# A long-convolution layer and a SwiGLU layer on one core: block 1's v loaded early into a y buffer, loads reordered, down weights in two pieces, opening planned anew

## The chip, the cores and the metric

The kernel runs on one core of a Trainium2 chip. The core has a matrix engine (PE, with its weight loads shown apart as PEld), a vector engine (DVE), an activation engine (ACT), a general engine (POOL) and a queue engine (SP) that issues transfers; 16 DMA engines move the data. The metric is device time in microseconds of one execution. Before the change the median of 13 runs is 350.85 us (349.63 to 352.18).

## The reference

Inputs are q, k, v of 2048 positions by 512 channels, a shift kernel of 4 taps and a long kernel of 2048 taps for each channel, and three weight matrices of a gated feed-forward layer (512 by 1792 twice, 1792 by 512). Everything is bf16. With x = q, two layers run, each of the form:

```python
x = x + A(layernorm(x), k, v)      # A: k_shift = 4-tap causal convolution of k
                                   #    kv = k_shift * v
                                   #    y = causal convolution of kv with ssm_k (by FFT) + kv * ssm_D
                                   #    returns layernorm(x) * y
x = x + B(layernorm(x))            # B: (silu(z @ w_gate) * (z @ w_up)) @ w_down
```

A's y doesn't depend on x: both layers use the same y, which is computed once. Only the normalised x that multiplies it differs.

## The kernel before, in words

The 2048 positions are cut into four blocks (c = 0 to 3) of 512. A block's convolution is done with transforms of 1024 points as matrix products: `spectrum_h` and `spectrum_x` bring a block of the long kernel and of kv to frequencies (H, X), `fold_h` combines two neighbouring kernel blocks to G, `product(i, j)` multiplies X of block i with G of block j on DVE and adds into Z of block i + j, and `inverse` brings Z back to y on PE. The opening does the same for block 0 in a shorter form (`half`, `direct`, `inverse_half`).

The feed-forward part runs in 16 units (layer, block, half), in the order of blocks, then layers, then halves. For 14 tiles of hidden features PE forms gate and up products into `pf` (112 matmuls of 256 columns for a unit), ACT applies Silu (`sg`) and copies the up part (`ht`), DVE multiplies both (line 903), and PE multiplies by the down weights into `pd` (line 916, 28 matmuls of 512 columns). `prologue(layer, c, h)` stands ahead of each unit: it normalises x, multiplies by y, adds, normalises again into z, and turns z into zT, in the first unit by PE (line 850, with copies by ACT and by DVE in line 853), in the others by transposing transfers that SP issues (line 827).

Nothing is issued in the order of the program. Each operation is recorded with its engine, an estimated cost, for transfers an estimated landing time (`lat`), and what it reads and writes (class `Plan`). `dues` gives each a due time, from the units' planned starts (`T0`, `DUR`) and slacks (`SLK`, `HSL`, `ASL`), stretched by group (`STRETCH`) and moved one by one by `SHIFTS`. `forward` then plays the estimates and so fixes one order for each engine's queue; at run time each engine works through its queue and waits on semaphores. `warm` puts small matmuls into planned holes of PE before 32 us. The lists `ST1`, `ST2`, `N_ACT`, `Z_ACT` say for which units statistics and normalisations run on ACT and not on DVE; `X_PE` says for which units x is added in `pd` by a matmul with the identity (line 875) instead of by DVE (line 955).

Buffers are rings: a load into a ring waits until the buffer's former readers are done. Ring `v` has one buffer, ring `y` two, `s8` ten. Block 1's v (`vt`) shares the one `v` buffer with block 0's, which PE reads until 21.3 us (line 468). Its 4-tap product with k is on DVE in line 519, from ACT's copy `ks` (line 518) of PE's shifted k. All transfers but one are issued by SP, one after the other; each uses one of eight semaphores in turn, and waits for the transfer eight before it. In the opening SP issues, in this order: taps, k of block 0, D, v of block 0, x of block 0, h of block 1, gate weights, the first half of the inverse table (a transposing transfer, line 1038), k of block 1 (transposing, line 370), down weights, the second half of the table, up weights, v of block 1 (line 396), then x, h and k for the next blocks.

Of the kernel before, what the change touches and what calls it, by code (L numbers as in the profile page):

```python
# [9 lines left out]
P = 128  # L10
# [3 lines left out]
ACT = mybir.ActivationFunctionType  # L14
# [2 lines left out]
LN_EPS = 1e-5  # L17

NB = 4
SLK = 25.57  # L20
H_DMA = lambda b: b in {2, 3}
ST1 = lambda l, c, h: (l, c, h) in {(0, 2, 0), (0, 3, 0), (1, 0, 0)}
ST2 = lambda l, c, h: (l, c, h) in {(0, 0, 0), (0, 2, 1), (1, 2, 1), (1, 3, 1)}
ASL = -167.89
K_ACT = lambda b: b in {2, 3}
PASSES = 1
PW = 1.2
PD_ACT, KV_ACT, ST_ACT = True, True, False
HSL = 49.11
Z_ACT = lambda l, c, h: (l, c, h) in {(0, 0, 1), (0, 3, 1), (1, 0, 0), (1, 0, 1), (1, 1, 1), (1, 2, 1)}  # L30
N_ACT = lambda l, c, h: (l, c, h) in {(0, 2, 0), (0, 3, 0), (1, 0, 1), (1, 1, 1), (1, 3, 0)}
GROUPS = (4, 4, 4, 2)
TINY = 0.2
SHIFTS = {8: -168.0, 9: -2.0, 32: -48.0, 36: -20.0, 48: -11.0, 50: -14.0, 52: 81.0, 66: -34.0, 67: 46.0, 70: 119.0, 78: 4.0, 83: 4.0, 89: 13.0, 99: 167.0, 102: 22.0, 106: -52.0, 109: -49.0, 130: 36.0, 136: 21.0, 161: 56.0, 176: -79.0, 186: -34.0, 240: 10.0, 241: 11.0, 248: 184.0, 250: 53.0, 258: -67.0}
X0, H0, I0 = 'direct', 'half', 'half'
Z_DUE = -45
X_PE = lambda l, c, h: (l, c, h) in {(0, 0, 0), (1, 2, 0)}
RINGS = {}
T0, FLOOR = 25.95, -54.39
DUR = [27.46, 52.65, 71.28, 66.57, 24.46, 6.54, 42.65, 47.17, 9.57, 39.07, 58.13, 31.81, 76.24, 78.5, 43.25, 33.23]  # L40
STRETCH = {1: {'PE': 2.47, 'DVE': 5.84, 'ACT': 16.37, 'POOL': 2535.84, 'SP': 127809.23}, 2: {'PE': 6.24, 'DVE': 2.14, 'ACT': 0.5, 'POOL': 1.22, 'SP': 3.69}, 3: {'PE': 13.63, 'DVE': 2.09, 'ACT': 1.5, 'POOL': 0.74, 'SP': 5.68}}
R = 4


# [230 lines left out]
def kernel(  # L275
# [14 lines left out]
    nc = tc.nc  # L290
    _, S, D = A_q.shape
# [25 lines left out]
    def new(ring, name, shape, dtype=BF16, parts=1):  # L317
        space = psp if ring in ("pf", "pc", "pd") else pool

        def make(slot):  # L320
            tag = f"{ring}{slot}" if ring != "one" else name
            return space.tile(list(shape), dtype, name=name, tag=tag)
        return plan.buf(ring, name, make, parts)

    def whole(name, shape, dtype=BF16, parts=1):
        return new("one", name, shape, dtype, parts)
# [20 lines left out]
    tapT, drow = whole("tapT", [P, KD, KS]), new("jk", "drow", [P, D])  # L347
    dg = whole("dg", [P, KD, KS, P], parts=KD * KS)
    fwd, inv = whole("fwd", [P, NT, P], parts=4), whole("inv", [P, NT, P], parts=2)
    wt = {"g": whole("wg_sb", [P, KD, F]), "u": whole("wu_sb", [P, KD, F]), "d": whole("wd_sb", [P, NF, D])}  # L350

    def fT(f, r):
        return fwd.t[:, BI[f, r], :]
# [11 lines left out]
    def load_k(b, due=None, after=()):  # L365
        if b == 0:
            kn[b] = new("s8", "kn", [P, R, D])
            return add("SP", 0.5, lambda: nc.sync.dma_start(out=kn[b].t[:], in_=k_t[:, b]), w=[kn[b]], lat=4.6, due=due)
        kT[b] = new("s8" if b == 1 else "k", "kTb", [P, KD, PADL + L])
        add("SP", 5.0 if b == 1 else 2.2, lambda: nc.sync.dma_start_transpose(out=kT[b].t[:], in_=k3[b * L - PADL:(b + 1) * L]),  # L370
            w=[kT[b]], lat=7.0 if b == 1 else 8.0, due=due, after=after)

    def transpose_k(b, ring, engs):

# [17 lines left out]
        return k_in  # L392

    def load_v(b, due=None, after=()):
        vt[b] = new("v", "vt", [P, R, D], parts=R)
        return add("SP", 0.6, lambda: nc.sync.dma_start(out=vt[b].t[:], in_=v_t[:, b]), w=[vt[b]], lat=4.5 if b else 5.9, due=due, after=after)

    def load_x(c, due=None, after=()):
        xs[c] = new("x", "xc", [P, R, D], parts=R + 2)
# [2 lines left out]
    def load_weights(which, due, after=()):  # L402
        if which in ("g", "u"):
            src = (B_w_gate if which == "g" else B_w_up).rearrange("(k p) f -> p k f", p=P)
        else:
            src = B_w_down.rearrange("(k p) d -> p k d", p=P)
        return add("SP", 0.6, lambda: nc.sync.dma_start(out=wt[which].t[:], in_=src), w=[wt[which]], lat=12.0, due=due, after=after)


    X, G, H, Y, Z = {}, {}, {}, {}, {}  # L410
# [451 lines left out]
    def ffn(unit):  # L862
# [18 lines left out]
        for fts in groups:  # L881
            n = len(fts)
            sg = new("sg", "sg", [P, n, W], parts=n // 2)
            ht = new("ht", "ht", [P, n, W], parts=n // 2)
            for o in range(0, n, 2):
                for which in ("g", "u"):
                    ps = new("pf", "pf", [P, D], F32)

                    def go(ps=ps, o=o, which=which, fts=fts):
                        for q in (0, 1):  # L890
                            ft = fts[o + q]
                            mm(ps.t[:, q * W:(q + 1) * W],
                               [(wt[which].t[:, kd, ft * P:(ft + 1) * P], zT.t[:, kd]) for kd in range(KD)])
                    add("PE", pe(2 * KD, W), go, r=[zT, wt[which]], w=[ps], due=(unit, (k + (which == "u") / 3) / pairs, 0.0, None))
                    if which == "g":
                        add("ACT", act(D), lambda ps=ps, o=o, sg=sg: nc.scalar.activation(  # L896
                            out=sg.t[:, o:o + 2, :], in_=ps.t[:], func=ACT.Silu), r=[ps], w=[(sg, (o // 2,))],
                            due=(unit, k / pairs, 1.0, "a"))
                    else:
                        add("ACT", act(D), lambda ps=ps, o=o, ht=ht: nc.scalar.copy(out=ht.t[:, o:o + 2, :], in_=ps.t[:]),  # L900
                            r=[ps], w=[(ht, (o // 2,))], due=(unit, k / pairs, 1.5, "a"))
                k += 1
            dve(n * W, lambda sg=sg, ht=ht: nc.vector.tensor_mul(out=ht.t[:], in0=ht.t[:], in1=sg.t[:]), [sg], [ht],  # L903
                due=(unit, k / pairs, 0.0, "h"))
            for o in range(HP):
                i = HP * h + o
                last = unit == LAST_UNIT and fts[-1] == NF - 1 and o == HP - 1
                split = unit == LAST_UNIT and o == HP - 1
                halves = (slice(0, D // 2), slice(D // 2, D))
                cols = [[cs] for cs in halves] if last else [halves] if split else [[slice(0, D)]]  # L910

                for css in cols:
                    def go(o=o, fts=fts, ht=ht, css=css):
                        for cs in css:
                            for q, ft in enumerate(fts):
                                nc.tensor.matmul((pds[o] if not cs.start else pds[HP]).t[:, cs], lhsT=ht.t[:, q, o * P:(o + 1) * P], rhs=wt["d"].t[:, ft, cs],  # L916
                                                 start=(ft == 0 and not xpe), stop=(ft == NF - 1))
                    add("PE", pe(n) if not last else pe(n, D // 2), go, r=[ht, wt["d"]],
                        w=[pds[o]] if not split else [pds[o], pds[HP]] if not last else [pds[HP if css[0].start else o]],
                        due=(unit, k / pairs, 2.0, None))  # L920
        if unit == LAST_UNIT:
# [81 lines left out]
            out=fwd.t[:, dst, :], in0=fwd.t[:, src, :], scalar1=-1.0, scalar2=None, op0=ALU.mult),  # L1003
            r=[(fwd, (n,))], w=[(fwd, (part,))])
    h1 = load_h(1, "SP", -57.5, after=[x0])
    wg = load_weights("g", -57, after=[h1])
    hs = transpose_h(0, "pf", (0, 2, 1, 3), False, ("DVE", "ACT"), drow)
    ev = spectrum("ev")
    if H0 == "half":
# [25 lines left out]
    k_in = transpose_k(0, "pc", ("ACT", "DVE"))  # L1035
    for n in range(2):
        sl = slice(n * NI, (n + 1) * NI)
        tabs = add("SP", 4.0, lambda sl=sl: nc.sync.dma_start_transpose(
            out=inv.t[:, sl, :], in_=fwd.t[:, sl, :].rearrange("p k f -> p (k f)")), r=[fwd], w=[(inv, (n,))], lat=5.5, due=-56.8,
            after=[wg, k_in])  # L1040
    load_k(1, -56.4, after=[tabs])
    load_weights("u", -56, after=[tabs])
    load_weights("d", -55, after=[tabs])
    shift_mul(0, "pf", False, due=-49)
    normed[0, 0, 0] = apply_norm(0, 0, on_act=True, due=-47)
    if H0 == "half":
# [24 lines left out]
        product(0, 0, [slot], False)  # L1071
    plan.grp = 1
    spectrum_h(1, "pf")
    v1 = load_v(1, after=[turned[1]] if 1 in turned else ())
    plan.grp = 0
    if I0 == "half":
        inverse_half(0, (0, 1))
# [16 lines left out]
    def conv(c):  # L1094
        if c >= NB:
            return
        plan.grp = c
        if c > 1:
            spectrum_h(c)
        fold_h(c)  # L1100
        spectrum_x(c)
        load_x(c, after=[v1])
        if c + 1 < NB:
            gate = list(first) if c == 1 else ()
            load_h(c + 1, after=gate)
            load_k(c + 1, after=gate)
            load_v(c + 1, after=gate)
        product(0, c)
        product(c, 0)
        inverse(c)  # L1110
        for i in range(1, c + 1):
            if i + c < NB:
                product(i, c)
                if i != c:
                    product(c, i)
# [53 lines left out]
```

## Time and profile before

| | us |
|---|---|
| median of 13 runs | 350.85 |
| the profiled execution: its time | 351.87 |
| the profiled execution: its span | 350.1 |
| busy in the span: PE, DVE, ACT, POOL | 340.2, 280.5, 259.6, 39.5 |
| first matmul of the first unit | 35.78 |
| longest wait of PE | 2.2 |
| loads issued, and time to landing: gate weights | 3.32, 12.1 |
| up weights | 21.09, 10.5 |
| v of block 1 | 21.79, 11.1 |

The profile is of one execution, taken by the hardware profiler. Its times count from the start of the span. A line of the list of waits gives who waited for whom, the sum, how often, and the longest. A line of the chain gives start, duration, engine and line, and how many instructions follow each other. A line of the timeline gives start, duration, engine, line, operation, output and inputs, shape and count, and in brackets the idle time before it with what ended it. PE's ends are modelled, so starts of neighbours say more than durations. The page's row PEclk is the clock that PE was granted, in tenths, in 40 equal slices. A few records of matmuls are missing from such a trace.

### The profile page before, as it was taken

To read this page: it belongs to the slowest core of one execution; us is meant where nothing else is said; L and a number is where in the kernel's file an instruction comes from. 1 tells how busy PE (TensorE), PEld (TensorE's weight loads), DVE (VectorE), ACT (ScalarE), POOL (GpSimd) and SP (SyncE) were. 2 spreads that over 40 slices of the span, in tenths; PEclk is the share of its full clock that TensorE was granted. 3 is DMA by queue.
4 is the path that set the end of the run, shared out by engine and by line. 5 is a ranking of instruction groups with operands and counts; after the bars stand their busy time and mean duration, and the time that the engine had idled before them with its cause. 6 is when DMAs were issued, how large, how long until landed. Compare 5 with 4: busy or idle time off the path is not lost.

```text
span 350.1 us, 6568 instructions
## 1 busy us (share of the span) xinstructions
PE 340.2 (97%) x2582; PEld 249.4 (71%) x2608; DVE 280.5 (80%) x471; ACT 259.6 (74%) x507; POOL 39.5 (11%) x46
## 2 busy tenths in 40 slices
PE   7997999999999999999999999999999999999996
PEld 7664676858588685858586777758586877777684
DVE  7897979999998997899999999999997523643120
ACT  6996896758779994938896989859983755648460
POOL 4100100111132000201212001101201000100000
PEclk9999699999999999999999999999999999999999
DMA  8999202010251116310113040120101130000200
GB/s 290 310 318 325 48 29 63 2 32 0 44 137 34 25 19 140 110 42 2 30 34 78 16 119 2 36 56 0 33 30 25 39 32 0 17 15 2 61 2 30
DMA packets 42073, 22.96 MB, mean 66 GB/s; under 512 B 33845, under 2 KB 39866, under 8 KB 42042
## 3 DMA queue, kind: packets, MB, share of 16 engines
q1 hardware_dynamic: 41370, 21.95, 24.3%
q10 hardware_dynamic: 672, 0.59, 0.6%
q8 instruction: 20, 0.33, 0.4%
q14 instruction: 11, 0.09, 0.1%
HBM read 12.33 MB, written 2.10 MB: 41 GB/s over the span
## 4 chain that ended last, share of the span: by engine, by line
PE 75%; DVE 13%; ACT 5%; DMA 4%; issue 2%; POOL 0%; DVEq 0%; POOLq 0%; ACTq 0%
PE pf L338 44%; PE pd L916 21%; PE ps L338 5%; DMA vt<-in_A_v_dram 3%; PE ps L468 2%; DVE ht L903 2%; DVE bnst L743 1%; DVE t L655 1%; DVE t L651 1%; DVE t L663 1%; ACT ht L900 1%; DVE ka L606 1%; PE wm L1135 1%; ACT sg L896 1%; DMA zT<-z 1%
## 5 line engine op out<-in xcount | busy, mean ns | idle before, releaser
L338 PE MATMUL pf<-zT,wg_sb 128*128 128x256 bf16 x896 | 117.8, 275 | 1.1 <-DVE zT L853 0.6
L338 PE MATMUL pf<-zT,wu_sb 128*128 128x256 bf16 x896 | 117.0, 274 | 0.0
L338 PEld LDWEIGHTS <-wg_sb 128*128 128x128 bf16 x896 | 88.1, 99 | 20.1 <-issue 1.3
L916 PE MATMUL pd<-wd_sb,ht 128*128 128x512 bf16 (+1 forms) x446 | 97.9, 372 | 1.2 <-DVE ht L903 0.3
L338 PEld LDWEIGHTS <-wu_sb 128*128 128x128 bf16 x896 | 88.1, 98 | 13.2
L896 ACT ACTIVATE sg<-pf 128x512 bf16<-128x512 f32 x112 | 67.3, 602 | 18.9 <-PE pf L338 17.6
L916 PEld LDWEIGHTS <-ht 128*128 128x128 bf16 x462 | 45.0, 98 | 47.4 <-DVE ht L903 0.9
L900 ACT CAST ht<-pf 128x512 bf16<-128x512 f32 x112 | 65.8, 587 | 15.1 <-PE pf L338 14.2
L903 DVE TENSOR_TENSOR ht<-ht,sg 128x1024 bf16<-128x1024 bf16 (+1 forms) x64 | 39.4, 620 | 26.9 <-ACT ht L900 26.9
L748 POOL TENSOR_TENSOR rstd<-ve,nhalf 128x2 f32<-128x2 f32 x24 | 27.5, 1146 | 219.3 <-DVE ve L746 205.5
L952 ACT CAST dn<-pd 128x512 bf16<-128x512 f32 x26 | 14.1, 591 | 34.5 <-PE pd L916 34.5
L743 DVE BATCH_NORM_STATS2 bnst<-xc 128x6 f32<-128x512 bf16 x48 | 31.4, 686 | 0.7
L651 DVE TENSOR_TENSOR t<-X,G 128x2048 bf16<-128x2048 bf16 x18 | 21.9, 1219 | 0.1
L655 DVE TENSOR_TENSOR t<-X,G 128x2048 bf16<-128x2048 bf16 x18 | 21.9, 1218 | 0.0
L955 DVE TENSOR_TENSOR xc<-xc,dn 128x1024 bf16<-128x1024 bf16 x13 | 8.9, 688 | 15.4 <-ACT dn L952 15.4
L429 ACT ACTIVATE X<-ps 128x512 bf16<-128x512 f32 x32 | 17.8, 603 | 0.2
L820 DVE TENSOR_TENSOR n<-n,Yk 128x1024 bf16<-128x1024 bf16 x15 | 10.4, 691 | 5.7 <-ACT n L793 3.8
L665 DVE TENSOR_TENSOR Z<-Z,t 128x2048 bf16<-128x2048 bf16 x12 | 14.7, 1222 | 0.2
L429 ACT ACTIVATE H<-ps 128x512 bf16<-128x512 f32 x24 | 13.2, 616 | 2.2 <-PE ps L338 2.1
L663 DVE TENSOR_TENSOR t<-t,t 128x2048 bf16<-128x2048 bf16 x12 | 14.6, 1220 | 0.1
L774 POOL TENSOR_TENSOR rstd<-ve,nhalf 128x2 f32<-128x2 f32 x8 | 7.8, 981 | 59.6 <-ACT ve L772 59.6
L768 ACT ACTIVATE jk<-xc,nm 128x512 bf16<-128x512 bf16 x16 | 11.5, 720 | 0.3
(108 smaller groups left out, 318.6 us busy)
## 6 DMA issues: line engine op xcount, KB each, us to landing
vt<-in_A_v_dram SPq DMA_DIRECT2D x4, 512.0 KB, 8.5
xc<-in_A_q_dram SPq DMA_DIRECT2D x4, 512.0 KB, 5.2
out_dram<-xc SPq DMA_DIRECT2D x15, 128.0 KB, 1.8
wg_sb<-in_B_w_gate_dram SPq DMA_DIRECT2D x1, 1792.0 KB, 12.1
wd_sb<-in_B_w_down_dram SPq DMA_DIRECT2D x1, 1792.0 KB, 8.2
wu_sb<-in_B_w_up_dram SPq DMA_DIRECT2D x1, 1792.0 KB, 10.5
hn<-in_A_ssm_k_dram SPq DMA_DIRECT2D x3, 512.0 KB, 7.9
hn<-in_A_ssm_k_dram ACTq DMA_DIRECT2D x1, 512.0 KB, 3.6
```

The lines of the kernel that those rows point to most:

```text
L338: nc.tensor.matmul(o, lhsT=lhsT, rhs=rhs, start=(n == 0), stop=(n == len(terms) - 1))
L429: add("ACT", act(D), lambda: nc.scalar.activation(out=view(), in_=ps.t[:], func=ACT.Copy, scale=scale), r=[ps], w=[(buf, keys)], conv=conv)
L651: dve(n * D, lambda t1=t1, part=part: nc.vector.tensor_mul(out=t1.t[:], in0=x.t[:, sl, 0, :], in1=g.t[:, sl, part, :]), [(x, key(slots, (0 ...
L655: dve(n * D, lambda t2=t2, part=part: nc.vector.tensor_mul(out=t2.t[:], in0=x.t[:, sl, 1, :], in1=g.t[:, sl, 1 - part, :]), [(x, key(slots ...
L663: dve(n * D, lambda t1=t1, t2=t2, comb=comb: nc.vector.tensor_tensor(out=t1.t[:], in0=t1.t[:], in1=t2.t[:], op=comb), [t2], [t1], conv=conv)
L665: dve(n * D, lambda t1=t1, part=part: nc.vector.tensor_add(out=z.t[:, sl, part, :], in0=z.t[:, sl, part, :], in1=t1.t[:]), [t1], [zk], con ...
L743: add("DVE", 0.6, lambda st=st, i=i: nc.vector.bn_stats(out=st.t[:], in_=xs[c].t[:, i, :]), r=[(xs[c], (i,))], w=[st])
L748: add("POOL", pw, lambda: nc.gpsimd.tensor_tensor(out=rstd.t[:], in0=ve.t[:], in1=nhalf.t[:].to_broadcast((P, n)), op=ALU.pow), r=[ve, nha ...
L896: add("ACT", act(D), lambda ps=ps, o=o, sg=sg: nc.scalar.activation(out=sg.t[:, o:o + 2, :], in_=ps.t[:], func=ACT.Silu), r=[ps], w=[(sg, ...
L900: add("ACT", act(D), lambda ps=ps, o=o, ht=ht: nc.scalar.copy(out=ht.t[:, o:o + 2, :], in_=ps.t[:]), r=[ps], w=[(ht, (o // 2,))], due=(uni ...
L903: dve(n * W, lambda sg=sg, ht=ht: nc.vector.tensor_mul(out=ht.t[:], in0=ht.t[:], in1=sg.t[:]), [sg], [ht], due=(unit, k / pairs, 0.0, "h"))
L916: nc.tensor.matmul((pds[o] if not cs.start else pds[HP]).t[:, cs], lhsT=ht.t[:, q, o * P:(o + 1) * P], rhs=wt["d"].t[:, ft, cs], start=(ft ...
```

## The change

Block 1's v gets a buffer of ring `y`, and its load is placed after h of block 1 and ahead of the gate weights. Both halves of the inverse table are now issued one after the other, ahead of k of block 1; then follow the up weights, and the down weights in two pieces (the first four feature tiles, then ten), which the down matmuls wait for separately. Landing times in the plan get new values. All the plan's constants and lists change with it, so each engine's order is another one through the whole kernel. On SP the opening's order is now: k of block 0, taps, D, v of block 0, x of block 0, h of block 1, v of block 1, gate weights, both halves of the table, k of block 1, up weights, the two pieces of the down weights, x of block 1, h, k and v of block 2. The warm-up matmuls go from 23 to 28, with 6 more ahead of H of block 1; `X_PE` gets the units (0, 0, 1) and (0, 2, 1).

```diff
-SLK = 25.57
+SLK = 22.46
-ST1 = lambda l, c, h: (l, c, h) in {(0, 2, 0), (0, 3, 0), (1, 0, 0)}
-ST2 = lambda l, c, h: (l, c, h) in {(0, 0, 0), (0, 2, 1), (1, 2, 1), (1, 3, 1)}
-ASL = -167.89
+ST1 = lambda l, c, h: (l, c, h) in {(0, 0, 0), (0, 1, 0), (0, 2, 0), (0, 3, 0), (0, 3, 1), (1, 0, 0)}
+ST2 = lambda l, c, h: (l, c, h) in {(0, 0, 0), (0, 2, 1), (1, 2, 1)}
+ASL = -171.35
-HSL = 49.11
-Z_ACT = lambda l, c, h: (l, c, h) in {(0, 0, 1), (0, 3, 1), (1, 0, 0), (1, 0, 1), (1, 1, 1), (1, 2, 1)}
-N_ACT = lambda l, c, h: (l, c, h) in {(0, 2, 0), (0, 3, 0), (1, 0, 1), (1, 1, 1), (1, 3, 0)}
+HSL = 66.69
+Z_ACT = lambda l, c, h: (l, c, h) in {(0, 2, 0), (0, 3, 1), (1, 0, 0), (1, 1, 0), (1, 1, 1), (1, 3, 0)}
+N_ACT = lambda l, c, h: (l, c, h) in {(0, 2, 1), (0, 3, 0), (0, 3, 1), (1, 1, 1), (1, 3, 1)}
-SHIFTS = {8: -168.0, 9: -2.0, 32: -48.0, ...
+SHIFTS = {11: 77.0, 31: 6.0, 34: -33.0, ...
-X_PE = lambda l, c, h: (l, c, h) in {(0, 0, 0), (1, 2, 0)}
+X_PE = lambda l, c, h: (l, c, h) in {(0, 0, 0), (0, 0, 1), (0, 2, 1), (1, 2, 0), (1, 3, 1)}
-T0, FLOOR = 25.95, -54.39
+T0, FLOOR = 85.74, -22.82
...
-"d": whole("wd_sb", [P, NF, D])}
+"d": whole("wd_sb", [P, NF, D], parts=2)}
...
-        vt[b] = new("v", "vt", [P, R, D], parts=R)
+        vt[b] = new("y" if b == 1 else "v", "vt", [P, R, D], parts=R)
...
+            for part, sl in enumerate((slice(0, GROUPS[0]), slice(GROUPS[0], NF))):
+                o = add("SP", 0.6, lambda sl=sl: nc.sync.dma_start(out=wt[which].t[:, sl], in_=src[:, sl]), w=[(wt[which], (part,))],
+                        lat=(8.0, 11.5)[part], due=due, after=after)
+            return o
...
-                    add("PE", pe(n) if not last else pe(n, D // 2), go, r=[ht, wt["d"]],
+                    add("PE", pe(n) if not last else pe(n, D // 2), go, r=[ht, (wt["d"], (0 if fts[0] == 0 else 1,))],
...
     h1 = load_h(1, "SP", -57.5, after=[x0])
-    wg = load_weights("g", -57, after=[h1])
+    v1 = load_v(1, -57.2, after=[h1])
+    wg = load_weights("g", -57, after=[v1])
...
-    load_k(1, -56.4, after=[tabs])
-    load_weights("u", -56, after=[tabs])
-    load_weights("d", -55, after=[tabs])
+    k1 = load_k(1, -56.4, after=[tabs])
+    wu = load_weights("u", -56, after=[k1])
+    wd = load_weights("d", -55, after=[wu])
...
-    v1 = load_v(1, after=[turned[1]] if 1 in turned else ())
...
-        load_x(c, after=[v1])
+        load_x(c, after=[wd])
```

## The prediction

> **What bounds the kernel now.** I read the page's first lines, then PE's waits, the chain, a table by stage, and the timelines.
>
> The page and its row of granted clock:
>
> ```profile
> PE 340.2 (97%) x2582; PEld 249.4 (71%) x2608; DVE 280.5 (80%) x471; ACT 259.6 (74%) x507; POOL 39.5 (11%) x46
> PEclk9999699999999999999999999999999999999999
> ```
>
> PE is the bound, with one hole: the fifth slice (35 to 44 us) has the clock at 6 tenths.
>
> PE's waits, and the chain:
>
> ```profile
> PE ptz L850 <- ACT ks L518: 2.2, 1, 2.2
> PE pf L338 <- DVE zT L853: 0.6, 1, 0.6
> ...
> 21.79 11.11 DMA vt<-in_A_v_dram
> 33.00 0.44 DVE vt L519
> 34.14 1.05 PE ptz L850 x8
> 35.78 7.89 PE pf L338 x48
> ```
>
> PE's long wait is one. The chain says what is behind it: block 1's v, issued at 21.79, lands at 32.9; the DVE product that needs it stands ahead of the two z of the first FFN unit.
>
> By stage (columns: stretch, then busy us of PE, PEld, DVE, ACT, POOL, then granted clock, DMA share, GB/s):
>
> ```profile
> 21.30:31.80 10.50, 10.32 (x106) 7.00 (x105) 9.21 (x21) 8.75 (x16) 0.69 (x1) 1.00 1.07 372
> 31.80:35.80 4.00, 1.19 (x10) 0.82 (x10) 2.66 (x8) 2.29 (x5) 0.00 (x0) 0.79 1.29 191
> 35.80:41.00 5.20, 5.20 (x25) 3.60 (x26) 5.13 (x7) 4.44 (x13) 1.03 (x1) 0.51 0.25 58
> 150.00:252.00 102.00, 101.19 (x737) 72.44 (x743) 100.97 (x149) 83.57 (x170) 13.36 (x10) 1.00 0.16 37
> 252.00:350.00 98.00, 94.20 (x722) 71.12 (x729) 43.13 (x86) 56.65 (x107) 6.45 (x8) 1.00 0.11 23
> ```
>
> Up to 35 us the DMA engines are full. After the hole PE runs 5.2 us at half clock. From 150 to 252 DVE is as full as PE, so whatever arrives late on DVE there decides too.
>
> PE's and DVE's timelines:
>
> ```profile
> 37.44 1.91 PE L338 MATMUL pf<-zT,wu_sb 128*128 128x256 bf16 x8
> 39.15 1.91 PE L338 MATMUL pf<-zT,wg_sb 128*128 128x256 bf16 x8
> 41.77 1.04 PE L338 MATMUL pf<-zT,wg_sb 128*128 128x256 bf16 x8
> 42.64 1.04 PE L338 MATMUL pf<-zT,wu_sb 128*128 128x256 bf16 x8
> ...
> 138.30 0.69 DVE L955 TENSOR_TENSOR xc<-xc,dn 128x1024 bf16<-128x1024 bf16 x1 [1.88 <-ACT dn L952]
> 228.00 0.73 DVE L798 TENSOR_SCALAR z<-xc,mv,rstd 128x512 bf16<-128x512 bf16 x2
> ```
>
> Eight matmuls take 1.71 us (37.44 to 39.15) and later 0.87 (41.77 to 42.64): the halved clock, in the record.
>
> **The change part by part.** Sums go against the profiled execution: span 350.1, its time 351.87, which is 1.0 above the median 350.85; I subtract differences from the median.
>
> *v of block 1 early.* It goes from thirteenth to seventh in SP's queue and is issued near 3.4. Before, v0, x0 and h1 landed at 7.8, 9.2 and 10.6 (5.9, 6.9 and 7.9 after issue): 1.4 us per 512 KB. So v1 lands near 12, over 17 us before its use. What it passes comes 1.4 us later: wg 16.8 instead of 15.4 (12.1 from 3.32), wanted at 34; the other transfers have their own line below. The order shows a new wait on wg, for the first h load (landed 4.3); wg is then issued 1 us later, covered by the same 17 us. With the wait gone, next in line on DVE are the statistics: ve ends 30.9, rstd takes 0.69 on POOL, so z could start near 31.8 instead of 33.7.
>
> *Warm-up matmuls, 23 to 28 and 6 more.* Five at 0.114 (2.63 for 23) put off the transposes by up to 0.57; at 6.8 the clock rises, which returns half: I take 0.4. The six stand in a hole that waits for ACT's copy of h: zero; without that cover 6 x 0.056 = 0.3.
>
> *PE's order up to the first FFN.* The same instructions, regrouped. From the end of the h1 transposes (22.2, now 22.6) stand 8 + 16 + 2 matmuls of 0.216, 64 tap matmuls of 0.06 to 0.065, eight transposes of 0.056: 9.9 to 10.2, and some 1.75 of waits: 0.8 for ACT's first copy of h, 0.3 and 0.55 for DVE's m, 0.1 for z. So PE, no longer DVE, sets the start: 34.4 instead of 35.78, **-1.4**, with the zT copy at 33.9 instead of 35.2.
>
> *The clock.* The largest hole I find on PE is now some 0.6 us against 2.4 before, so no half clock: the 24 matmuls from 35.78 to 40.86 take 24 x 0.109 = 2.6 instead of 5.1, **-2.5**. The Trainium skill ("TensorE: Matmul & The Clock Gate", Why this matters for your kernels) asks only to avoid idle gaps over about 3 us. Here 2.4 us was followed by the halving, so the trace is stricter; by the page's rule the change would have nothing to win here, and the sum would be 2.5 worse.
>
> *Transposes of the inverse tables and k.* Now consecutive on SP: 5.1 + 4.3 + 6.1 from 5.2 on, so k of block 1 is fully issued near 20.8 instead of 16.1. Its landing isn't shown before. Block 2's landed 2.7 after SP was done (14.2 from 23.84, 11.5 on SP), the first table 6.3 after: 23.5 to 27.1. PE wants it near 24.1: zero to +3.0. I take zero, since little is queued ahead of it then; the upper end stays in the range. wu follows: issued 21.1 as before, 10.5 to land at most, 31.6, wanted at 36.
>
> *wd in two pieces.* One more issue on SP (0.59) ahead of x1, h2, k2, which nobody wants before 70 us: zero. Its parts land at the latest with the old last load of this stretch, 36 to 38, wanted near 43 and 48. v2 now waits for v0's readers (done by 21.3) and no longer for v1's, so it can't hold the zT transposes behind it.
>
> *The y slot.* Y0 has the other slot; Y1 needs one only after X1 is formed (50.2 before) and is written past 80 us: zero.
>
> *X_PE on two more units.* Two matmuls each, 4 x 0.216 = **+0.9** on PE. DVE loses two adds of 0.69.
>
> *ST, Z, N lists and the new order.* In all DVE has -2.9 us, ACT +3.1 (two sums and two squares of rows more, 0.71 to 0.81 each; ACT has 83.6 of 102 us busy in the full stretch, which covers them). Place matters more than totals. I summed DVE's instructions in list order, each at the spacing of its row, from the zT copy to the second z of unit (layer 1, block 2, half 0), just where before has no slack (z ends 228.7, zT lands 232.46, PE starts 232.59). Before: 287 instructions, 184.5 us, done in 193.5, so 9.0 were idle. After: two products more (2 x 1.135), one ht (0.60), two n (0.73), less two bn with their small ones (1.56) and one add (0.69): 185.8. Of the 9.0 idle, the 1.88 at 138.3 waits for PE, and PE is ahead now: I take 7.1. Then z ends 33.9 + 185.8 + 7.1 = 226.8, zT lands 3.8 later at 230.6. PE's matmuls up to that unit are 194.2 (193.3 and the 0.9): 228.6. It waits 2.0, where before it had lost 0.9 by then: **+1.1**. The ends: 9.0 idle costs +3.0, 5.1 or less costs -0.9. Past 252 DVE is at 43 of 98 us and hides its part.
>
> Sum: -1.4 - 2.5 + 0.9 + 1.1 = -1.9: span 348.2, time **348.9**.
>
> The page "DMA: Bandwidth & Descriptors" (Issuing engines are not separate DMA queues) says all loads interleave on the same 16 engines, so an early load is paid by others. The trace agrees (DMA share 1.07 to 35 us); by the slack in the sums above, only k pays.
>
> **The rivals.**
>
> *DVE gives nothing back* (the new order fits the earlier PE): PE alone counts, -1.4 - 2.5 + 0.9 and up to -0.5 for a faster start: 347.3 to 347.8. For it: DVE totals fall by 2.9 and past this unit the sums are 1.6 to 6 smaller than before. Against: between 150 and 252 DVE has 1 us free of 102.
>
> *DVE takes everything* (the slower side): the order asks 4 to 6 us more of DVE ahead of the products ht of units (1,1,0) and (1,1,1), and if DVE then also stands idle for PE or ACT as it did, 9.0 us, z ends at 228.7 as before: no change, 350.8. From 9.7 idle it decides for slower, 1 us for each: with 11, 352.8. For it: static order, 83.6 of 102 on ACT and 3.1 more to come. Against: the waits of 35 to 150 hang on PE, which is ahead.
>
> *The opening stalls again* (k late by up to 3.0, a hole like the old one, half clock 2.5): gain gone, 350.5 to 352.
>
> *v1 was hidden anyway*: no; its landing ends the only long wait of PE. Without any effect of it the time would be 350.85 + 0.9.
>
> **How the numbers follow.** A change under 0.2% (0.7 us) can hardly be told from none. Forecast 0.42 (own range 347.9 to 350.1); nothing given back 0.20; DVE as idle as before, no change, 0.12; DVE more idle, slower, 0.16; opening stalls, slower, 0.10. Faster 0.62, same 0.12, slower 0.26. The range reaches down to a start at 33.9 without any stall, 346.9, and up to the late k or 10.4 us idle, 352.2.
>
> **What would show it.** Right: v1 landing near 12; no PE hole over 1 us between 22 and 35; clock 9s in the fifth slice; first pf near 34.4; PE waiting about 2 us in all before the unit (1,2,0), for ht or zT. Wrong: PE waiting on taps for k near 24; a 5 or 6 in PEclk; many PE waits for DVE's ht between 40 and 60 or 160 and 230, in all over 4 us; the ACT queue late for sg and ht in the first unit, which the half clock used to cover.

## The result, and the profile after

The changed kernel takes 347.46 us (median of 11 runs, 347.22 to 349.50) against 350.72 (48 runs, 349.38 to 352.22): a ratio of 0.9922, interval 0.9904 to 0.9939. The forecast was 348.9. A twelfth execution was disturbed (2048 us), and it was the profiled one; so the lines of the changed kernel below are of the same kernel, unaltered, profiled again in a later run (e9 below: span 345.6, its time 347.32).

The times of the changed kernel don't spread evenly. Over this series and two later ones (e1 and e9), 23 executions without the disturbed one, 14 lie between 347.2 and 348.3, most of them at 347.2 to 347.5, and 9 between 349.1 and 349.7. The profile below is one of the 14; e1's is one of the 9.

The page, its busy times and the row of granted clock:

```profile
PE 337.5 (98%) x2595; PEld 248.6 (72%) x2623; DVE 277.4 (80%) x465; ACT 262.3 (76%) x515; POOL 39.6 (11%) x46
PEclk9999999999999999999999999999999999999999
```

The hole in the fifth slice is gone. So is PE's wait of 2.2 us for v; its list of waits begins, apart from the start of the kernel, with small ones:

```profile
PE ps L338 <- ACT hs L495: 0.4, 1, 0.4
PE pt L1025 <- DMA tapR<-in_A_shift_k_dram: 0.3, 1, 0.3
PE ps L338 <- ACT X L433: 0.3, 1, 0.3
PE pt L491 <- DMA hn<-in_A_ssm_k_dram: 0.2, 1, 0.2
```

Two of these, for the taps and for the first h, stand in the first six microseconds; they come up again.

The chain of work that ended last (start, duration, engine and line) no longer has a transfer of v in it; between 30 and 33 us it goes:

```profile
30.09 1.05 PE ps L338 x16
31.15 0.05 issue
31.20 1.24 PE ps L735 x5
32.44 0.24 PE ptz L854 x4
32.70 0.58 ACT zT L859
```

PE's own work runs into the transposes of z without a hole. By stage, in the stretches that were used before (the last one shorter, as the span is):

```profile
21.30:31.80 10.50, 9.77 (x106) 6.96 (x107) 10.07 (x24) 9.41 (x18) 0.80 (x1) 1.00 1.06 376
31.80:35.80 4.00, 4.00 (x36) 2.93 (x35) 3.97 (x8) 3.90 (x11) 0.00 (x0) 1.00 1.24 221
35.80:41.00 5.20, 5.15 (x47) 4.48 (x46) 5.17 (x7) 4.92 (x12) 1.67 (x1) 1.00 0.37 108
150.00:252.00 102.00, 101.58 (x759) 74.76 (x765) 98.40 (x147) 87.43 (x176) 14.81 (x11) 1.00 0.16 37
252.00:345.00 93.00, 89.84 (x688) 67.71 (x692) 37.17 (x78) 55.50 (x103) 5.13 (x7) 1.00 0.09 21
```

The granted clock is 1.00 in every row, where it was 0.79 and 0.51 in two of them. From 150 to 252 us DVE has 98.4 busy us where it had 101.0. PE's and DVE's timelines around the first FFN matmul, and one later add:

```profile
32.28 0.61 PE L854 MATMUL ptz<-ident,z 128*128 128x128 bf16 x8
32.72 0.38 PE L735 MATMUL ps<-m,inv 128*128 128x512 bf16 x1
32.94 0.59 PE L879 MATMUL pd<-xc,ident 128*128 128x512 bf16 x2
33.49 1.03 PE L338 MATMUL pf<-zT,wg_sb 128*128 128x256 bf16 x8
34.36 1.04 PE L338 MATMUL pf<-zT,wu_sb 128*128 128x256 bf16 x8
```

```profile
31.55 0.74 DVE L802 TENSOR_SCALAR z<-xc,mv,rstd 128x512 bf16<-128x512 bf16 x2 [0.25 <-POOL rstd L752]
32.20 0.75 DVE L523 TENSOR_TENSOR vt<-ks,vt 128x512 bf16<-128x512 bf16 x2
32.92 0.42 DVE L857 COPY zT<-ptz 128x512 bf16<-128x512 bf16 x1
...
131.83 0.69 DVE L959 TENSOR_TENSOR xc<-xc,dn 128x1024 bf16<-128x1024 bf16 x1 [0.69 <-ACT dn L956]
```

The first FFN matmul starts at 33.49 (35.78 before), eight of them take 0.87 from the start, and the add waits 0.69 where it waited 1.88.

So the 4.5 us between the two profiled spans (350.1 and 345.6) are made up as follows. The start: 33.49 against 35.78, -2.3. From there to PE's last matmul: 308.7 us (342.21 - 33.49) against 310.9 (346.69 - 35.78), -2.2. The rest after PE's last matmul is 3.4 before and 3.3 now. I call these two parts the start and the body. The profiled execution of before was 1.0 above the median of its runs, and the medians differ by 3.3. Its half clock is longer than in most: its mean granted clock is 0.990. Of the 56 executions of the old kernel in the later series, 5 have 0.990 (median 352.5), 33 have 0.995 (350.8) and 18 have 0.999 or more (350.2). So most executions of before lost about half as long to half clock as the profiled one, and 18 nearly nothing.

### The profile page after: what moved, and what is told of

Read it like the earlier page. It is cut to its first block, busy times and chain, and to the rows that moved or that the text cites. A ratio compares the mean times of both kernels' runs of the same rounds, so it can differ in the third digit from the quotient of the medians.

```text
span 2046.3 us, 6592 instructions
## 1 busy us (share of the span) xinstructions
PE 2015.2 (98%) x2595; PEld 838.6 (41%) x2623; DVE 284.5 (14%) x465; ACT 280.8 (14%) x515; POOL 33.2 (2%) x46
## 4 chain that ended last, share of the span: by engine, by line
PE 98%; issue 1%; ACT 0%; POOL 0%; POOLq 0%
PE pf L338 58%; PE pd L920 28%; PE ps L338 7%; PE ps L472 2%; PE ps L735 1%; PE wm L1139 1%; PE pt L491 1%; PE pd L879 1%; PE pt L382 0%; PE ptz L854 0%; ACT X L433 0%; ACT xc L933 0%; POOL ident masks.py:199 0%; PE pt L1025 0%; POOL ident masks.py:197 0%
## 5 line engine op out<-in xcount | busy, mean ns | idle before, releaser
L338 PE MATMUL pf<-zT,wg_sb 128*128 128x256 bf16 x896 | 635.6, 1046 | 2.8 <-ACT X L433 1.9
L338 PE MATMUL pf<-zT,wu_sb 128*128 128x256 bf16 x896 | 635.1, 1045 | 0.0
L920 PE MATMUL pd<-wd_sb,ht 128*128 128x512 bf16 (+1 forms) x444 | 581.5, 1664 | 16.9 <-issue 16.9
L338 PEld LDWEIGHTS <-wg_sb 128*128 128x128 bf16 x896 | 289.3, 323 | 351.6 <-issue 351.6
L338 PEld LDWEIGHTS <-wu_sb 128*128 128x128 bf16 x896 | 289.7, 323 | 308.9 <-issue 308.9
L920 PEld LDWEIGHTS <-ht 128*128 128x128 bf16 x462 | 149.7, 324 | 415.5 <-issue 408.7
L907 DVE TENSOR_TENSOR ht<-ht,sg 128x1024 bf16<-128x1024 bf16 x64 | 40.0, 625 | 1059.2 <-ACT ht L904 1032.1
L338 PE MATMUL ps<-hs,fwd 128*128 128x512 bf16 x38 | 57.6, 1679 | 1.9 <-issue 1.9
L338 PE MATMUL ps<-dg,kTb 128*128 128x128 bf16 x128 | 43.9, 715 | 0.0
L472 PE MATMUL ps<-vt,fwd 128*128 128x512 bf16 x31 | 42.4, 1711 | 0.9 <-issue 0.9
L338 PE MATMUL ps<-vt,fwd 128*128 128x512 bf16 x22 | 34.1, 1709 | 0.0
```

The source lines that it names most:

```text
L338: nc.tensor.matmul(o, lhsT=lhsT, rhs=rhs, start=(n == 0), stop=(n == len(terms) - 1))
L472: add("PE", pe(2), lambda ps=ps, n=n, terms=terms: [nc.tensor.matmul(ps.t[:], lhsT=fT(f, r), rhs=rows.t[:, r, :], start=(n + o == 0), stop ...
```

## The experiments

Two questions were open: which part of the change brings the 2.3 of the start and the 2.2 of the body, and where the second group of times, 2 us higher, comes from. Each kernel was compared with the kernel before on the same chip in the same series, whose medians were 350.75 (e1 to e4), 350.72 (e5 to e8) and 350.58 (e9 to e12).

### e1: the changed kernel again

No edit.

> The changed kernel once more, for a profile at the usual clock. All theories: time 347.2 to 347.8. My theory (early v ends PE's hole and the half clock; DVE's order takes some of it back): v of block 1 lands near 12, first pf between 33.9 and 34.9, no half clock after it, and PE waits 1.5 to 2.5 us in all for DVE or zT before unit (1,2,0). Rival (PE counts alone): PE waits less than 0.7 us there, and the first pf stands at 34.4 or later.

Measured: 349.21 (347.28, 347.47, and four from 349.16 to 349.71), ratio 0.9928 (0.9901 to 0.9955). The profiled execution is the longest, 349.71. Its body is 308.71 (344.62 - 35.91), the same as in the profile above; its first FFN matmul starts at 35.91 instead of 33.49, 2.4 later, and 2.4 is what the two times differ by. So the two groups differ in the start alone, and the body keeps its gain in both. The median lies above the 347.2 to 347.8 that all theories expected. PE has no wait for DVE or zT over 0.1 us before unit (1,2,0), as the rival (PE counts alone) expected. The opening on PE, e1 first and then the execution of e9:

```profile
5.10 0.29 PE L1025 MATMUL pt<-ident,tapR 4*128 4x4 bf16 x4 [0.22 <-DMA tapR<-in_A_shift_k_dram]
5.55 1.47 PE L491 MATMUL pt<-ident,hn 128*128 128x128 bf16 x12 [0.16 <-DMA hn<-in_A_ssm_k_dram]
...
8.95 1.49 PE L338 MATMUL ps<-hs,fwd 128*128 128x512 bf16 x3
```

```profile
5.07 0.29 PE L1025 MATMUL pt<-ident,tapR 4*128 4x4 bf16 x4 [0.32 <-DMA tapR<-in_A_shift_k_dram]
5.58 0.86 PE L491 MATMUL pt<-ident,hn 128*128 128x128 bf16 x12 [0.22 <-DMA hn<-in_A_ssm_k_dram]
...
7.39 1.89 PE L338 MATMUL ps<-hs,fwd 128*128 128x512 bf16 x7
```

The work begins at the same time, but twelve transposes take 1.47 us in one and 0.86 in the other. The trace's record of the clock says why: the first rise to full clock is at 10.7 us in e1 and at 4.5 in e9 (6.8 in the profile of before).

### e2: the old kernel, only v early

```diff
...
+        place[vt[1]] = 1
+        vt[1].make = lambda slot: pool.tile([P, R, D], BF16, name="vt", tag="y1")
+        seq.remove(v1)
+        seq.insert(seq.index(h1) + 1, v1)
...
```

All orders and lists are the old ones; only the load of v moves to the seventh place on SP, into the y buffer.

> The old kernel with its old order on every engine; only the load of block 1's v moves to seventh place on SP, into a y buffer. My theory: the early v alone carries the gain: first pf near 33.9 instead of 35.78, clock full, and no extra 0.9 us of matmuls, so 346.3 to 348.0. Rival (the gain is the new plan's, its orders and lists): 349.5 to 350.8. Rival (the old body is so full on DVE that it takes everything): 350.0 to 350.8, with the first pf early all the same and PE waiting 3 us or more for DVE before unit (1,2,0).

Measured: 349.37 (348.79 to 352.93), ratio 0.9969 (0.9941 to 0.9996): a fraction of the change, and in none of the three ranges. v lands at 12.0, as intended. But PE has a new longest wait, here from its list of waits and then in its timeline:

```profile
PE ps L731 <- DMA inv<-fwd: 3.5, 1, 3.5
```

```profile
22.48 2.24 PE L338 MATMUL ps<-dg,kTb 128*128 128x128 bf16 x32
28.23 1.28 PE L731 MATMUL ps<-m,inv 128*128 128x512 bf16 x3 [3.50 <-DMA inv<-fwd]
```

The second half of the inverse table, which in the old order is issued behind k of block 1 and the down weights, now lands at 28.2 and PE waits for it. The start is 37.43, 1.65 later than before; the body, 308.9, has all of its gain (the profiled execution, 351.5, is one of the longer ones). The early v moves the stall from v to the table. (The clock falls in the profiled execution too, for 3.4 us, but it is back at 32.3, ahead of the body. Eight of the twelve executions have a mean clock of 0.999 or more and take 348.8 to 350.1.)

### e3: the old kernel, only the half clock taken away

```diff
+            if o is self.fill_at:
...
+                        warm(ring, i, self.fill_n)
...
```

42 small matmuls stand in the hole ahead of the transposes of z.

> The old kernel with 42 small matmuls (2.3 us) ahead of the transposes of z, where PE stands idle for v. Nothing else moves: v lands at 32.9 as before, the first pf stands at 35.8 to 36.2. If the hole is what halves the clock, the clock stays full. If PE counts alone, 2.5 us are gained: 348.0 to 348.6. If DVE binds the middle (my theory), DVE starts no earlier than before and gives almost nothing: 349.6 to 350.8. If the halving has nothing to do with the hole, it is still there and the time is 350.7 to 351.2.

Measured: 350.79 (350.18 to 351.36), ratio 0.9993 (0.9977 to 1.0009): no change, although the page shows full clock throughout. From PE's waits, and PE's timeline:

```profile
PE pf L345 <- DMA zT<-z: 1.5, 2, 1.3
```

```profile
31.91 2.51 PE L1145 MATMUL wm<-ident 128*128 128x128 bf16 x42
...
231.63 1.03 PE L345 MATMUL pf<-zT,wg_sb 128*128 128x256 bf16 x8 [1.32 <-DMA zT<-z]
```

At the second unit PE is 2.3 ahead of before, and it loses 1.3 of that at unit (1,2,0), where it waits for zT. DVE doesn't hold it there: DVE's zT copy starts at 34.91 instead of 35.21, and z of that unit ends 191.6 us after that, at 226.46, 2.3 earlier than before (228.73). What comes in between is SP, which starts the transposes of z only after four other transposes, of `kc` (k with its taps applied, for a later block). SP's timeline, before first and then here:

```profile
223.51 5.13 SPq L610 DMA_TRANSPOSE kc<-ka  x4
228.75 2.51 SPq L827 DMA_TRANSPOSE zT<-z  x2
```

```profile
221.23 6.43 SPq L617 DMA_TRANSPOSE kc<-ka  x4
227.78 2.51 SPq L834 DMA_TRANSPOSE zT<-z  x2
```

The four take 5.12 to 5.14 us in every other trace (the disturbed execution aside) and 6.43 here, so z is taken up 1.3 us late, which is PE's wait. Before, zT landed 3.7 us after z's end; with that it would have landed at 230.2, and PE was ready at 230.3. One of the four took 2.55 us instead of 1.26. In these five microseconds the trace has one load of instructions (16 KB, from 223.2 to 224.6), and before has none in the same stretch. The 42 added matmuls move such loads, so all twelve executions may have met it; that is argued, for only one was traced.

So e3 shows that filling the hole keeps the clock full. It doesn't show that the half clock is worth nothing, nor the expected cause (DVE binds the middle), although the time fits that expectation: the filler brought a wait of its own, at SP.

### e4: the changed kernel, v late

```diff
+        seq.remove(v1)
+        seq.insert(seq.index(wd) + 1, v1)
```

The new orders stay; v keeps the y buffer, but is loaded behind the down weights.

> The changed kernel, every engine in its new order; only the load of block 1's v goes back behind the down weights on SP (its y buffer stays). My theory: v lands near 32.5, PE's hole of some 2 us and the half clock come back, first pf near 35.5: 1.1 later and 2.5 of half clock, less what the waits for DVE in the middle (1 to 2 us) take up: 349.3 to 351.4. Rival (the gain is the new plan's): 347.3 to 348.3.

Measured: 349.42 (348.58 to 349.71), ratio 0.9944 (0.9925 to 0.9964). v lands at 32.8 as before the change, and PE waits in front of the transposes of z again, this time for z, since DVE's product with v stands ahead of it:

```profile
PE ptz L854 <- DVE z L802: 1.2, 1, 1.2
```

The start is 35.50; the body is 308.65. The time lies in the range of the expectation, but the half clock that was to come back did not: the new order halves the hole by itself (1.2 instead of 2.4), and the clock stayed full. So the new order alone keeps the body's gain, and the early v is worth 2.0 us of start, against the 14 executions near 347.4.

### e5: the old kernel with v, the tables and the weights in the change's order on SP

```diff
...
+        for o in (wd, wu, k1, tabs, v1):
+            seq.remove(o)
+        at = seq.index(h1) + 1
+        seq.insert(at, v1)
+        at = seq.index(tab0) + 1
+        seq[at:at] = [tabs, k1, wu, wd]
...
```

v goes into the y buffer as in e2. Every engine but SP keeps the old order, the old lists, the down weights in one piece.

> The old kernel in its old order, with SP's opening in the order of the change: v of block 1 seventh, then both halves of the inverse table, k of block 1, up weights, down weights (in one piece). Theory (a full repair of the opening needs v and the tables, and the rest is decided by DVE's old order in the middle): no PE wait over 1 us between 22 and 34, first pf 33.3 to 34.2, full clock, and PE waits 2 us or more for DVE before unit (1,2,0): 348.6 to 349.6. Rival (PE counts alone, the new body order is worth nothing): the change's time less its 0.9 us of added matmuls, 346.3 to 347.3.

Measured: 347.33 (347.11 to 348.01, all six), ratio 0.9912 (0.9894 to 0.9931): the whole gain. The start is 33.32, the body 308.70. PE's longest waits, besides the start of the kernel:

```profile
PE pf L338 <- DVE zT L853: 0.7, 1, 0.7
PE ptz L850 <- DVE z L798: 0.4, 1, 0.4
PE pd L916 <- DVE ht L903: 0.3, 1, 0.3
PE pf L338 <- DMA zT<-z: 0.2, 1, 0.2
```

So the order of five loads, with v in the y buffer, is the change. New due times, five lists, two more units with x by matmul and the split of the down weights add nothing that these runs can tell from zero. The expectation that the old order of DVE would hold the time back fell: from the zT copy to z of unit (1,2,0) DVE takes 191.3 us here, 193.5 before and 191.2 in the changed kernel.

### e6: the changed kernel, taps ahead of k of block 0

The changed kernel issues k of block 0 (512 KB) first on SP, at 0.72, the moment ACT issues the first h (512 KB); before, the small taps load came first.

```diff
+        seq.remove(k0)
+        seq.insert(seq.index(taps) + 1, k0)
```

> The changed kernel with one swap: the load of the taps goes out before that of block 0's k, as in the old kernel, so that the first h load has the DMA engines for itself for 0.4 us longer. Theory (the change makes the first h land 1.2 us late, and the two groups of times, 347.4 and 349.4, come from when the clock rises after that): h lands at 4.0 to 4.4, PE's first transposes stand at 5.0 to 5.2 instead of 5.55, and the upper group is gone or rare: median 346.7 to 347.3. Rival (the groups have another cause): h early, the two groups still there with the same shares.

Measured: 347.22 (347.03 to 347.79, all six), ratio 0.9908 (0.9889 to 0.9926). The first h lands at 4.2 instead of 5.5, the clock rises at 4.7, the first FFN matmul starts at 32.94. No execution falls in the higher group, as the theory expected.

### e7: the same with 23 first warm-up matmuls

```diff
+        n = 23 if n == 28 else n
```

> As the run before, and only 23 first warm-up matmuls instead of 28. Theory (the clock rises by the window of time in which PE is busy, and transposes count): first transposes at 4.5, 346.2 to 347.0. Rival (warm-up matmuls carry the rise): the clock rises 3.4 us later in more of the runs, and the upper group comes back: median 347.5 to 349.5.

Measured: 347.52 (346.86 to 347.88, all six), ratio 0.9912 (0.9893 to 0.9930). The median lies above the theory's 346.2 to 347.0, and the upper group, which the rival expected, isn't there either. In the profiled execution the clock rises at 7.3, later than in e6 (4.7) and e12 (5.5). The five matmuls more are worth nothing that can be told from zero when h comes early.

### e8: the changed kernel, x of units (0,0,1) and (0,2,1) added by DVE

```diff
+        by_dve = (layer, c, h) in {(0, 0, 1), (0, 2, 1)}
...
+                            nc.vector.tensor_add(out=x.t[:, rows, :], in0=x.t[:, rows, :], in1=dns[0][:])
```

This takes away the four matmuls that the prediction priced at +0.9.

> The changed kernel, but units (0,0,1) and (0,2,1) add x on DVE (ACT copies to dn, one add of 0.69 each) and not by matmuls. PE counts alone in the new order: 0.9 less, so 346.4 to 346.7 in the lower group. DVE decides the middle: the 1.4 more on DVE cost 0.5 to 1.4 and the matmuls' 0.9 is not won: 347.3 to 348.5.

Measured: 348.19, again in two groups, eight of 347.92 to 348.35 and four of 349.74 to 350.40; ratio 0.9943 (0.9922 to 0.9964). The lower group is 0.5 to 0.6 slower than the changed kernel's. PE's list of waits has a new first line behind the start of the kernel:

```profile
PE pf L338 <- DMA zT<-z: 0.4, 1, 0.4
```

The zT of unit (1,0,1) now lands 0.05 before PE starts on it, after that wait; in the changed kernel it had landed 0.17 before. The body is 309.35 against 308.72, 0.6 longer with 0.9 less to do for PE. So what hangs on the two adds costs PE some 1.5 us. PE falls behind e9 at five places, by 0.1 to 0.6 us each, of which the list shows only the longest. That these are DVE's lateness is argued: the time lies where the expectation with DVE deciding the middle had it (347.3 to 348.5).

### e9 to e12: where the two groups come from

The four ran together. e9 is the changed kernel, unaltered. e10 has 34 first warm-up matmuls instead of 28, which fill the hole ahead of the late first h. e11 is e5 with the taps load moved behind k of block 0, so that the first h is late there. e12 is e6 again.

```diff
+        n = 34 if n == 28 else n
```

for e10, and on top of e5's edit for e11

```diff
+        seq.remove(taps)
+        seq.insert(seq.index(k0) + 1, taps)
```

> The changed kernel once more, unaltered, beside its variants. Both theories (late first h; chance alone) expect two groups of times, near 347.2 to 347.6 and near 349.1 to 349.7, with a mean between 347.8 and 349.0. If the profiled execution falls in the lower group, its clock should rise by 7.3 us at the latest and the first matmul of the first unit should start near 33.7; in the upper group near 35.9 with the rise after 9 us. A single group would say that the two groups were a matter of the chip or the moment.

> The changed kernel with 34 warm-up matmuls in the opening instead of 28 (6 x 0.114 = 0.7 us more, up to about 5.57, when the first h has landed at 5.5). Theory A, it is the two short holes of PE (0.22 and 0.16 us) between warm-ups and transposes that make the clock rise one step later: the holes are filled, so all executions fall in one group, at 347.2 to 347.8, and the rise comes before 7.5 us. Theory B, it is the late start of the transposes as such, because matmuls with h arrive too late to count in the same stretch: the two groups stay, 347.4 to 347.8 and 349.2 to 349.9.

> The old kernel with v, tables, k1 and weights in the change's order (which had 347.33, all six executions between 347.1 and 348.0), and now also k of block 0 ahead of the taps, as the change has it. If the order of these two small loads delays the first h and with it the clock, h lands near 5.5 instead of 4.6 and a part of the executions goes up by about 2 us, to 349.0 to 349.9; the median then lies between 347.4 and 349.6. If the groups belong to the changed kernel's other parts (28 warm-ups, order on PE), all executions stay between 347.1 and 348.2.

> The changed kernel with the taps load ahead of k of block 0, a second time. With the late first h as cause: one group again, 347.0 to 347.9, median 347.2 to 347.4, 0.2 to 2 us below the changed kernel's median in this same call by the share of upper executions there. If the six executions of the first time were luck: one or more at 349.0 to 349.8.

Measured: e9 347.57 (five of 347.25 to 348.30, one of 349.65), ratio 0.9926 (0.9900 to 0.9953). e10 347.72 (347.29 to 348.21, all six), 0.9917 (0.9899 to 0.9935). e11 349.63 (349.25 to 350.31, all twelve), 0.9973 (0.9960 to 0.9985). e12 347.24 (346.62 to 347.94, all six), 0.9906 (0.9884 to 0.9927). e9 has two groups again, and its traced execution, one of the lower, has the early rise (4.5 us) and the start (33.49) that were expected. e10 is one group with a rise at 5.3, as theory A has it. In e11 all executions went up and not a part. e11's start is 36.08 against e5's 33.32, with a body of 308.7 in both. PE's opening in e11, and then in e10:

```profile
1.72 2.64 PE L1136 MATMUL wm<-ident 128*128 128x128 bf16 x23 [1.72 <-POOL ident masks.py:199]
5.06 0.29 PE L1020 MATMUL pt<-ident,tapR 4*128 4x4 bf16 x4 [0.70 <-DMA tapR<-in_A_shift_k_dram]
5.55 1.90 PE L487 MATMUL pt<-ident,hn 128*128 128x128 bf16 x16 [0.20 <-DMA hn<-in_A_ssm_k_dram]
```

```profile
1.72 3.77 PE L1140 MATMUL wm<-ident 128*128 128x128 bf16 x34 [1.72 <-POOL ident masks.py:199]
5.43 0.29 PE L1025 MATMUL pt<-ident,tapR 4*128 4x4 bf16 x4
5.65 0.86 PE L491 MATMUL pt<-ident,hn 128*128 128x128 bf16 x12
```

What sorts the runs whose v and tables come early is the time from the last warm-up matmul to the first transpose of h, in which PE has only four tiny matmuls for the taps:

| kernels | first h lands | that time on PE, us | first rise of the clock | executions up to 348.4 | at 349.1 and above |
|---|---|---|---|---|---|
| e5, e6, e7, e12 | 4.2 to 4.6 | 0.15 to 0.26 | 4.7 to 7.3 | 24 | 0 |
| e10 | 5.5 | 0.16 | 5.3 | 6 | 0 |
| the change (with e1, e9), e8 | 5.5 | 0.66 to 0.84 | 4.5; 9.3 and 10.7 | 22 | 13 |
| e11 | 5.5 | 1.19 | 10.6 | 0 | 12 |

(Times on PE and rises are of the profiled executions, one for each kernel, e1 and e9 for the change.) e11 shows that the order of two loads is enough: two places swapped on SP, and the median is 2.3 us above e5's, with no execution below 349.2. e10 shows that the late h costs nothing as such; the idle PE ahead of it does. e10 has only six executions; at the change's share (14 of 23 in the lower group) six of six in the lower one would come by chance in some 5 of 100 series. Together with e11's twelve of twelve on the other side, I take the hole as the cause. Within the third row the length of the hole doesn't sort the executions: e9, with 0.84, is in the lower group, e1, with 0.66, in the higher.

That makes e6 (and e12) the better version: 347.2, with no execution in the higher group. In e9's and e12's common series the means are 347.9 and 347.3. e5, with far fewer edits, is as good.

## Why the prediction was right or wrong

Right in sign, 1.4 us too high in size. Between the profiled executions the miss is larger: the forecast span was 348.2, e9's is 345.6. Of these 2.6 us, 0.9 are the start, 1.1 the share that DVE was to take back, and 0.6 a further gain of the body. The medians differ by less because the median of before carries less half clock than the profiled execution that the sum was made from.

*v early, its landing and what it passes.* Right: v lands at 11.2 (e9) and 12.0 (e1), forecast near 12; the gate weights at 16.6 and 17.1, forecast 16.8; PE has no hole over 0.6 us between 22 and 33 (the longest in e9 is 0.4). The forecast put the zero on k of block 1, with an upper end of 3.0 us. k was issued by 18.0 (e9) and not 20.8, and PE never waits for it: zero was right. The two halves of the inverse table were passed over as part of one sum on SP, and that is where a plan with v alone fails (e2, 3.5 us). That the change moves the second half from behind the down weights to the front is as much its gain as the early v; the forecast priced it as a possible loss only.

*The start, -1.4.* Mis-sized: measured -2.3 in the e9 profile (33.49 against 34.4 forecast), which is of the 14 executions in the lower group, and +0.1 in the e1 profile, which is of the other 9. The term's two parts: the warm-ups, taken at 0.4, left no delay, since transposes of h of block 1 begin at 21.32 in e9 and at 21.31 before (though the first h came 1.2 later and the clock rose 2.3 earlier there, so the three can't be told apart); and PE's waits on the way, taken at 1.75, are about 0.9 (33.49 less 22.22, less 10.05 of matmuls and 0.34 of the six warm-ups). For the other 9, the step that failed is the one on the warm-ups. It took the first h as landing at 4.3, as before, and the clock as rising at 6.8, as before. That k of block 0 goes ahead of the taps was told as part of the change and not priced: h lands at 5.5, and in 9 executions of 23 the start is lost again; in e1's the clock rises at 10.7 us.

*The clock, -2.5.* Right for the profiled execution: full clock, 8 matmuls in 0.87 from the first one on. Against the median it is too much: by the groups of before above, a mean clock of 0.990 goes with 352.5, 0.995, which most executions have, with 350.8, and a full one with 350.2. No run prices the half clock alone; in e3, which was to do so, the filler brought a wait of 1.3 us at SP.

*x by matmul on two more units, +0.9.* The matmuls are there, but e8 shows that without them the kernel is 0.5 to 0.6 slower, not 0.9 faster. The forecast booked them as a cost of PE, and of the two adds saved only one (0.69) in DVE's sum.

*DVE gives back, +1.1.* This step failed. It took DVE's idle time of 9.0 us, kept 7.1 of it, and had z of unit (1,2,0) end 192.9 us (185.8 and 7.1) after the zT copy, with PE waiting 2.0. Measured: 191.2 us in both profiles of the changed kernel, PE waits nowhere for it, and zT of that unit lands 1.49 us before PE starts (0.13 before). PE's side of the sum was off too: PE comes to that unit 195.7 us after its first FFN matmul and not 194.2, with 51 matmuls of the convolution on the way where before had 46, so zT had more time. The body is 308.7, where 310.9 - 2.5 + 0.9 is 309.3: instead of +1.1 it gains 0.6 more, from the waits of before (0.43 for an ht at 229 us, 0.33 at 252). The reason on DVE's side is its waits over 0.25 us in that stretch, which sum to 5.74 before and 2.38 after. I had taken the add at 138.3 (1.88) as the one that goes because PE is ahead. In e5, where PE is ahead and the order is old, that one stays (1.88); what goes there are three waits just after the half clock (for n at 46.9, 1.23; for ht at 50.5, 0.39; for X at 51.5, 0.30), 1.92 in all. They are gone in e3 as well, where the filler kept the clock full and DVE's order is the old one: they were the half clock's echo, by way of ACT. In the changed kernel both kinds shrink: of those three 0.28 is left, and the add waits 0.69.

So the case that came is the rival *DVE gives nothing back*, 347.3 to 347.8, which had 0.20: start earlier, full clock, matmuls added, PE alone counting. What spoke for it in the forecast (DVE's totals 2.9 lower) was right; what spoke against it, 1 us free of 102, was a reading of one window of the old profile, from 150 to 252, while the waits that shrank lie ahead of that window, between 46 and 148 us. That its number came is in part luck: the start and the body gained 0.9 and 0.6 more than its sum, and the half clock, which the sum took at 2.5, costs most executions of before much less. *DVE takes everything*, *the opening stalls again* and *v was hidden anyway* did not come. A relative of the second did, in a place that the forecast didn't look at: not k of block 1 late at 24 us, but the first h late at 5.5 us, for 9 executions in 23, at 2 us.

## What to carry to other kernels

When one late load ends the only long wait, list what lands next behind it and what the move pushes back: here the load alone was worth 0.3%, and with the next late one (the second half of the table) moved up too, and the loads behind it in the change's order, 0.9%, in an otherwise untouched kernel. Before an engine's idle time is carried over to a new plan, trace each of its waits back to its root; those that lead to the stall that is removed go with it. And give the first loads of a kernel in the order in which PE needs them: a hole of well under a microsecond in the first window of work can cost 2 us through the clock, in some executions and not in others, so compare distributions, not only medians.

## What was not expected of the hardware

The clock moves in steps. In every trace with a record of the clock the stretches of full and half clock are, apart from the last, whole multiples of 3.413 us (27.307 and 6.827 before, 3.41 in e2, 337.919 and 341.333 in e1 and e9), and the phase against the kernel's start differs from one execution to the next. The Trainium skill ("TensorE: Matmul & The Clock Gate", What's actually happening) states such a free-running window of 3413 ns, and the traces agree. By the runs here a step has to be filled for the most part before the clock rises at its end. Steps with 0.3 us or less without work were followed by a rise (e5, e7, e10); e11's, with 1.19, was not. (The four small matmuls for the taps are counted as no work in these figures.) Between them it is a close thing: e4's step (2.95 to 6.36) held 0.66 of the hole ahead of h and was followed by a rise, and so was e9's (1.04 to 4.45), with 0.68 before the first matmul; e1's (3.85 to 7.26) with 0.66 and e8's (2.47 to 5.89) with 0.69 were not. That puts the limit near 0.7 of 3.4 us, as an estimate from these rows, but by a hundredth or two the rows contradict each other, and with the four matmuls counted as work they don't sort at all (0.38 and 0.41 in e1 and e8, 0.68 in e9). It would also explain the two groups: whether the hole falls into the deciding step, and how much of it, is settled by the phase. That is argued; no run set the phase.

For a fall, less than a whole idle step is enough: a hole of 2.4 us (before) and one of 3.5 (e2) were followed by half clock in the traced executions. The hole of 1.2 in e4 wasn't; it lay across the end of a step, with 0.9 on one side and 0.3 on the other. The phase seems to decide here as well: 18 of 56 executions of before and 8 of 12 of e2 have a mean clock of 0.999 or more, so there the hole, if it was as long, was followed by no such fall. In the two traces the longer hole cost the shorter stretch, 3.4 us against 6.8. In e2 PE was busy from 28.2 on without a break; before, the first step at half clock also held the 0.6 us in which PE waited for the copy of zT, which would explain a second one. That reading is argued from two traces, and not tested; by their mean clock most executions of before lost one step, too.

The second: of two loads of 512 KB issued by different engines within 0.01 us of each other, the one that PE wanted first came last. The first h (issued by ACT) lands at 5.5 us when SP issues k of block 0 in the same moment, and at 4.0 to 4.6 when a small load goes ahead and k follows 0.45 us later; k itself lands at 4.3 in the first case and at 5.2 to 5.9 in the second. What is moved there is only who comes first.
